# 384 columns of half the rows of one w_down tile, loaded earlier in 18 small transfers over a few DMA engines

## The chip, the cores and the metric

One core of a Trainium2 chip runs the kernel. The metric is the device time of one execution in microseconds, lower is better. Before the change three runs took 227.02, 227.11 and 227.11 us, so the median is 227.11 us.

## The reference

One token of a decoder layer with a parallel attention branch and feed-forward branch, all in fp32. Attention reads a window of 4096 cached keys and values of four key/value heads; the feed-forward part is a gated GELU.

```python
xn = _layernorm(x, axis=-1)                       # x: 1 x 1 x 1024
return x + _A_ref(xn, k_cache, v_cache, wq, wo) + _B_ref(xn, w_gate, w_up, w_down)
...
q = xn @ wq                                       # 1024 x 4096, 32 heads of 128
p = _softmax(q @ k.T * 128 ** -0.5, axis=-1)      # last 4096 rows of the caches
A = (p @ v) @ wo                                  # wo: 4096 x 1024
B = (gelu(xn @ w_gate) * (xn @ w_up)) @ w_down    # 1024 x 3584, w_down: 3584 x 1024
```

## The kernel before

**The work.** There is one token, so every weight is read once and used for one product of a vector and a matrix. The kernel is a stream of 94.38 MB from HBM through one buffer, `ring`, of 128 partitions by 32768 fp32 columns (128 KB of each partition). The table `PLAN` (line 269) gives the order of the loads, the column at which each starts, and the load whose readers must be done before it may be issued: wq in two halves, K and V of two heads, half of w_gate, K and V of the other two heads, the rest of w_gate, w_up in three parts, wo in two halves (`o 0`, `o 1`), and w_down in three parts (`d 0`, `d 1`, `d 2`). All of these loads are issued by SyncE (SP in the profile), in this order, by `load` (line 313); `used` (line 335) issues what stands behind a load once its consumer's instructions have been written. A DMA waits on SP until the readers of the columns that it overwrites are done, so a late reader holds the whole SP queue.

**A tile.** Rows of w_down and wo are laid out so that a partition holds whole neighbouring rows: `grouped` (line 292) puts row `p * rows + t` of a part into partition `p` as its tile `t`, 1024 columns wide. So w_down has 28 tiles: 16 in `d 0`, 8 in `d 1` and 4 in `d 2`. `PIECES` (line 27) cuts `d 1` into two transfers of 4 tiles each, and `d 2` into one of two tiles (24 and 25), one of tile 26, and two of half of tile 27. These six, and `d 0` in one piece, are the seven w_down transfers of the profile.

**Who consumes what.** A tile is either multiplied on TensorE (PE) by a column of `oz` or `hz`, accumulating in `out_p`, or on VectorE (DVE) by `add_scaled` (line 435): out_part = out_part + tile * column, one scalar per partition. In wo (`outputs`, line 697) even tiles go to PE and odd ones to DVE. In w_down (`downs`, line 707) the six tiles of `KEPT` in `d 0` go to DVE and all others to PE; `out_part` itself is summed over partitions by PE with `units` just ahead of tile 24. The last half tile goes to `last_p`, is added to `y` as `y_last`, and is stored.

**The hidden vector.** `hidden` (line 651) stands between the two halves of wo on PE and DVE: it turns the gated vector, which lies along rows of `copies` (tile `kT` in the profile), into columns of `hz`, one for each w_down tile, with 28 small matmuls into `tp` and seven DVE copies into `hz`.

**Synchronisation** is derived by the class `Flow`: it notes what each instruction reads and writes, and gives each the waits that it needs. Every instruction is issued from its line 238, so nearly every row of the profile has the line L238, and rows are told apart by their tiles.

Of the kernel before, what the change touches and what calls it, by code (L numbers as in the profile page):

```python
# [5 lines left out]
F32 = mybir.dt.float32  # L6
# [5 lines left out]
P = 128  # L12
D = 1024
# [4 lines left out]
DF = 3584  # L18
NR = 4
NJ = D // (NR * P)  # L20
NB = 512
# [10 lines left out]
GELU_C = math.sqrt(2.0 / math.pi)  # L32

ROW = (31, 32, 95, 96)
SIZES = {"tp": NB, "acc": 2 * NB, "part": 8 * NB, "rows": 2 * NB}


# [203 lines left out]
class Pool:  # L241
# [6 lines left out]
    def tile(self, shape, dtype, name, tag=None, bufs=1):  # L248
# [5 lines left out]
        if key not in self.made:  # L254
            alloc = self.nc.alloc_psum_tensor if self.space == "psum" else self.nc.alloc_sbuf_tensor
            width = SIZES.get(tag, size)
            self.made[key] = (alloc(f"{tag}_{n}", [P, width], dtype), width)
# [18 lines left out]
]  # L276

# [1 line left out]
def decode_layer(nc, x, k_cache, v_cache, wq, wo, w_gate, w_up, w_down, out):  # L279
    consts = stream = work = Pool(nc.nc, "sbuf")  # L280
    psum = Pool(nc.nc, "psum")

    def fours(w, jj):
        return w[NR * P * jj:NR * P * (jj + 1), :].rearrange("(p r) n -> p r n", r=NR)


    def windows(cache, i):
        pair = cache[0, 2 * i:2 * i + 2, SK - WIN:, :]
        return pair.rearrange("g (p j) d -> p g (j d)", p=P // 2)


    def grouped(w, start, rows):
        return w[start:start + P * rows, :].rearrange("(p t) n -> p t n", p=P)


    def source(kind, i):
        if kind == "q":
            return fours(wq, i)
        if kind == "g":
            return fours(w_gate, i)  # L300
        if kind[0] == "u":
            return fours(w_up, i)[:, {"u": slice(NR), "ua": slice(2), "ub": slice(2, NR)}[kind]]
        if kind in "kv":
            cache = k_cache if kind == "k" else v_cache
            return windows(cache, i)
        if kind == "o":
            return grouped(wo, P * WIDE * i, WIDE)
        return grouped(w_down, P * sum(DOWN[:i]), DOWN[i])

    ring = stream.tile([P, RING], F32, name="ring")  # L310
    loaded = {}

    def load(key, at):
        kind, i = key
        src = source(*key)
        if kind in "kv":

            loaded[key] = dst = ring[:, at:at + RING // 4]
            if kind == "v":
                nc.sync.dma_start(dst, src)  # L320
            else:
                for odd in range(2):
                    nc.sync.dma_start(dst[odd:P:2], src[:, odd])
            return
        rows, n = src.shape[1:]
        loaded[key] = ring[:, at:at + rows * n]
        dst = loaded[key].rearrange("p (t n) -> p t n", n=n)
        pieces = PIECES[i] if kind == "d" else (0, rows)
        for t, end in zip(pieces, pieces[1:]):
            cuts = 2 if key == ("d", 2) and end == rows else 1  # L330
            for cut in range(cuts):
                cols = slice(cut * n // cuts, (cut + 1) * n // cuts)
                nc.sync.dma_start(dst[:, t:end, cols], src[:, t:end, cols])

    def used(key):

# [12 lines left out]
    for c in (0, 2):  # L349
        nc.scalar.dma_start(  # L350
            x_out[ROW[c]:ROW[c] + 2, :].rearrange("c (h n) -> c h n", h=2), x_in[c:c + 2]
        )

    ident = consts.tile([P, P], F32, name="ident")
# [12 lines left out]

    hz = consts.tile([P, TD + 1, 32], F32, name="hz")
    nc.vector.memset(hz, 0.0)
    oz = consts.tile([P, HQ + 1, 32], F32, name="oz")  # L370
    nc.vector.memset(oz, 0.0)
    units = consts.tile([P, 2, 32], F32, name="units")
# [62 lines left out]
    def add_scaled(total, w, factor, first):  # L435

        if first:
            nc.vector.tensor_scalar(total, w, factor, None, op0=ALU.mult)
        else:
            nc.vector.scalar_tensor_tensor(total, w, factor, total, op0=ALU.mult, op1=ALU.add)  # L440
# [51 lines left out]
    m = work.tile([P, HKV], F32, name="m")  # L492
# [135 lines left out]
    copies = (h_sb[:, 0:4], h_sb[:, 4:6])  # L628
    rows = (P, 32 * (NA - 4))
# [21 lines left out]
    def hidden():  # L651

        h_p = small("h_p")
        kept = ((0, 16, 0, 4), (1, 8, 0, 2), (1, 4, 2, 1))
        t = at = 0
        for b, count, c, n in kept:
            k = rows[b]
            m = NB // count  # L660
            flat = copies[b][:k].rearrange("p a n -> p (a n)")
            for i in range(count):
                nc.tensor.matmul(
                    h_p[:, at + i:at + n * count:count], flat[:, i:P * count:count],
                    ident[:k, 32 * c:32 * (c + n):32], start=True, stop=True,
                )
            for own in range(n):
                r = slice(m * own, m * own + m)
                cols = slice(at + count * own, at + count * own + count)
                nc.vector.tensor_copy(hz[r, t:t + count, 31], h_p[r, cols])  # L670
            t, at = t + count, at + n * count


    out_p = psum.tile([P, CO], F32, name="out_p", tag="out")
    out_part = work.tile([P, D], F32, name="out_part")
# [5 lines left out]
    def store(h, rows):  # L681

        dst = out.rearrange("a b (h c n) -> h (a b c) n", h=2, c=4)[h]
        for queue, c in ((nc.sync, 0), (nc.scalar, 2)):
            stores.append(len(nc.ops))
            queue.dma_start(dst[c:c + 2], rows[ROW[c]:ROW[c] + 2, :])

    def accumulate(p, z, t, w, start, stop):
        w = w.rearrange("p (h c n) -> p c h n", c=4, n=CO // 2)
        z = z.rearrange("p t m -> p (t m)")  # L690
        for c in range(4):
            at = 32 * (t + c) + 31 - ROW[c]
            nc.tensor.matmul(
# [13 lines left out]
    def downs():  # L707

        nonlocal mark
        tiles = [loaded["d", i][:, n * D:(n + 1) * D] for i in range(3) for n in range(DOWN[i])]  # L710
        for t in KEPT:
            add_scaled(out_part, tiles[t], hz[:, t, 31:32], False)
        order = [t for t in range(DOWN[0]) if t not in KEPT]
        half = DOWN[0] + DOWN[1] // 2
        for t in [*order[:6], *range(DOWN[0], half), *order[6:], *range(half, TD - 4)]:
            accumulate(out_p, hz, t, tiles[t], False, False)
        accumulate(out_p, units, 0, out_part, False, False)
        for t in range(TD - 4, TD - 1):
            accumulate(out_p, hz, t, tiles[t], False, False)

        n = CO // 2
        t, wt = TD - 1, tiles[TD - 1]
        accumulate(out_p[:, :n], hz, t, wt[:, :NB], False, True)
        mark = len(nc.ops)
        nc.vector.tensor_add(y, out_p, x_out)
        store(0, y[:, :n])
        last_p = small("last_p")[:, :n]
        accumulate(last_p, hz, t, wt[:, NB:], True, True)
        nc.vector.tensor_add(y_last, y[:, n:], last_p)
        store(1, y_last)  # L730
# [4 lines left out]
    half = RING // 8  # L735
    for key, _, _ in PLAN:
        kind, i = key
        if kind == "q":
            project("q", i, loaded.pop(key), range(NR), 8)
        elif kind == "k":  # L740
            kn = loaded.pop(key)
            if i == 0:
                projected("q", 8)
                q_sb = query_rows()
            transpose_keys(2 * i, kn[:, :half], range(8), (1, 4, 6))
            if i == 0:
                queries(q_sb)

            s = scores(2 * i)
            transpose_keys(2 * i + 1, kn[:, half:], range(4), ())  # L750
            exponentials(2 * i, s)
            transpose_keys(2 * i + 1, kn[:, half:], range(4, 8), (4, 5, 7))
            s = scores(2 * i + 1)
        elif kind == "v":
            vn = loaded.pop(key)
            pT = transpose_probs(2 * i)
            exponentials(2 * i + 1, s)
            values(2 * i, pT, vn[:, :half])
            values(2 * i + 1, transpose_probs(2 * i + 1), vn[:, half:])
            if i == 1:  # L760
                maxima()
        elif kind == "g":
            project("g", i, loaded.pop(key), range(NR), NA)
            if i == 1:
                state = factors()
                projected("g", NA)
                gelu()
        elif kind in ("ua", "ub", "u"):
            taken = {"ua": (0, 1), "ub": (2, 3), "u": range(NR)}[kind]
            project("u", i, loaded.pop(key), taken, NA)  # L770
            if kind == "ua":
                normalizers(*state)
            elif kind == "ub":
                heads()
        elif kind == "o":
            if i == 0:
                projected("u", NA)
                gated()
            outputs(i)
            if i == 0:  # L780
                hidden()
        elif i == 2:
            downs()
        used(key)
# [26 lines left out]
```

## Time and profile before

| | |
|---|---|
| runs shown | 227.02, 227.11, 227.11 us; median 227.11 us |
| the profiled execution, its time | 227.12 us |
| its span, from first to last instruction | 225.2 us |
| mean granted TensorE clock | 0.795 |
| PE, DVE, ACT, POOL busy | 56%, 48%, 13%, 0% of the span |
| read from HBM | 94.38 MB, 419 GB/s over the span |

A row of the timeline gives the start and the length in us, then engine, line, operation, output tile and input tiles, shapes, how many instructions were merged, and in brackets how long the engine had been idle and what ended it. "PEld" is the weight load of a matmul, "SPq" is an instruction of SP's own sequencer such as the issue of a DMA. The windows view has one row for each stretch: its length, the busy time of each engine with the number of instructions in parentheses, the granted TensorE clock, the mean busy share of the core's 16 DMA engines, and GB/s. The share is made by the packets that start in the stretch, so a short stretch can be a few hundredths off. In the DMA view, q1 is the queue of SP's transfers, q10 that of ScalarE's, and "instruction" are the core's own fetches of instructions, which run on the same 16 engines.

### The profile page before, as it was taken

The page shows a single profiled execution, that of the slowest core. Times are in us where ns is not written, and L with a number is a line of the kernel's source. Part 1 is how long each engine was busy: PE and PEld are TensorE (multiplying, and loading weights), DVE is VectorE, ACT ScalarE, POOL GpSimd, SP SyncE. Part 2 cuts the span into 40 slices and gives each one's busy share as a digit, 9 for nine tenths or more (in the row PEclk, how much of TensorE's full clock was granted, in tenths as well). Part 3 has the DMA queues.
Part 4 walks back from the last instruction along what each step waited for, and adds up shares of the span by engine and source line. Part 5 has one row for each costly group of instructions (what it writes and reads, how often), then busy time and mean ns, then how long its engine had stood idle before and what let it go on. Part 6 is the DMA issues. An engine that isn't in the chain of part 4 may idle for free.

```text
span 225.2 us, 2481 instructions
## 1 busy us (share of the span) xinstructions
PE 125.4 (56%) x1107; PEld 66.0 (29%) x1107; DVE 107.7 (48%) x133; ACT 28.2 (13%) x54; POOL 0.7 (0%) x6
## 2 busy tenths in 40 slices
PE   0120910538799992999736553236308989700975
PEld 0010200103646651755511110001004887300441
DVE  7030920591215382345139589239608813950931
ACT  2020000002407410464300310000000000000000
POOL 1000000000000000000000000000000000000000
PEclk9999975596959999799988958558955755765699
DMA  9899889799997999998999999999999999998993
GB/s 373 373 396 536 372 384 547 343 402 463 438 489 336 432 439 451 402 516 377 461 390 418 433 463 418 479 422 466 399 442 454 407 442 442 410 442 361 425 404 141
DMA packets 2954, 94.52 MB, mean 420 GB/s; under 512 B 367, under 2 KB 383, under 8 KB 769
## 3 DMA queue, kind: packets, MB, share of 16 engines
q1 hardware_dynamic: 2920, 94.38, 97.5%
q8 instruction: 8, 0.13, 0.2%
q10 hardware_dynamic: 24, 0.01, 0.0%
q14 instruction: 2, 0.01, 0.0%
HBM read 94.38 MB, written 0.00 MB: 419 GB/s over the span
## 4 chain that ended last, share of the span: by engine, by line
DMA 68%; DVE 20%; PE 9%; ACT 1%; issue 1%; SPq 0%; DVEq 0%
DMA ring<-in_B_w_gate 26%; DMA ring<-in_A_wq 18%; DMA ring<-in_A_wo 13%; DVE part L238 13%; DMA ring<-in_B_w_down 11%; PE tp L238 6%; DVE out_part L238 3%; PE out L238 3%; DVE rows L238 2%; DVE g_sb L238 1%; ACT kT L238 1%; DVE hz L238 1%; PE acc L238 0%; DVE kT L238 0%; SPq L238 0%
## 5 line engine op out<-in xcount | busy, mean ns | idle before, releaser
L238 PE MATMUL acc<-ring,xz 128*32 128x512 f32 x176 | 31.5, 811 | 39.4 <-DMA ring<-in_A_wq 22.3
L238 DVE SCALAR_TENSOR_TENSOR part<-ring,xz,part 128x3584 f32<-128x3584 f32 (+1 forms) x9 | 37.2, 4129 | 23.2 <-DMA ring<-in_A_wq 12.5
L238 PEld LDWEIGHTS acc<-ring,xz 128*32 128x32 f32 x176 | 7.1, 139 | 59.6 <-issue 25.6
L238 PE MATMUL tp<-ident,ring 128*128 128x128 f32 x128 | 20.9, 308 | 6.2 <-DMA ring<-in_A_k_cache 4.0
L238 PE MATMUL out<-ring,hz 128*32 128x256 f32 (+1 forms) x176 | 12.3, 426 | 14.2 <-DMA ring<-in_B_w_down 14.0
L238 PEld LDWEIGHTS tp<-ident,ring 128*128 128x128 f32 x128 | 15.5, 156 | 15.7 <-DMA ring<-in_A_k_cache 4.9
L238 DVE SCALAR_TENSOR_TENSOR out_part<-ring,oz,out_part 128x1024 f32<-128x1024 f32 x15 | 19.3, 1284 | 0.5
L238 DVE COPY kT<-tp 128x512 f32<-128x512 f32 x12 | 8.2, 690 | 20.0 <-PE tp L238 20.0
L238 PE MATMUL out<-ring,oz 128*32 128x256 f32 x128 | 12.1, 562 | 9.5 <-DMA ring<-in_A_wo 9.5
L238 ACT ACTIVATE kT<-tp 128x512 f32<-128x512 f32 x20 | 11.6, 596 | 25.8 <-PE tp L238 25.5
L238 PE MATMUL tp<-ident,kT 128*128 128x4 f32 (+2 forms) x56 | 13.1, 366 | 1.3 <-DVE hz L238 1.3
L238 PEld LDWEIGHTS tp<-ident,kT 128*128 128x128 f32 (+1 forms) x56 | 12.8, 319 | 1.9 <-DVE hz L238 1.5
L238 PE MATMUL acc<-part,units 128*32 128x512 f32 x44 | 7.2, 741 | 9.2 <-DVE part L238 9.2
L238 PEld LDWEIGHTS out<-ring,hz 128*32 128x32 f32 x176 | 5.7, 123 | 21.0 <-DMA ring<-in_B_w_down 17.0
L238 DVE SCALAR_TENSOR_TENSOR out_part<-ring,hz,out_part 128x1024 f32<-128x1024 f32 x6 | 7.7, 1285 | 8.0 <-DMA ring<-in_B_w_down 7.8
L238 DVE TENSOR_SCALAR part<-ring,xz 128x3584 f32<-128x3584 f32 (+1 forms) x3 | 6.5, 2171 | 10.4 <-DMA ring<-in_A_wq 7.4
L238 PEld LDWEIGHTS out<-ring,oz 128*32 128x32 f32 x128 | 5.4, 160 | 16.1 <-DMA ring<-in_A_wo 10.4
L238 PE MATMUL s<-kT,qz 128*32 128x512 f32 x64 | 9.4, 714 | 0.0
L238 DVE TENSOR_REDUCE m<-s 128x2 f32<-128x1024 f32 x4 | 4.9, 1224 | 7.5 <-PE s L238 7.5
L238 PE MATMUL o<-ring,pT 128*32 128x128 f32 x256 | 7.8, 274 | 1.0 <-ACT pT L238 1.0
L238 PEld LDWEIGHTS o<-ring,pT 128*32 128x32 f32 x256 | 6.7, 110 | 1.9 <-ACT pT L238 1.9
L238 PE MATMUL tp<-ident,x_rows 2*128 2x2 f32 x4 | 0.6, 252 | 10.5 <-DMA x_rows<-in_A_x 10.5
(88 smaller groups left out, 68.9 us busy)
## 6 DMA issues: line engine op xcount, KB each, us to landing
ring<-in_B_w_gate SPq DMA_DIRECT2D x2, 7168.0 KB, 29.5
ring<-in_A_k_cache SPq DMA_DIRECT2D x4, 2048.0 KB, 18.1
ring<-in_A_v_cache SPq DMA_DIRECT2D x2, 4096.0 KB, 25.3
ring<-in_B_w_up SPq DMA_DIRECT2D x2, 3584.0 KB, 22.5
ring<-in_B_w_up SPq DMA_DIRECT2D x1, 7168.0 KB, 26.0
ring<-in_B_w_down SPq DMA_DIRECT2D x2, 2048.0 KB, 21.6
ring<-in_B_w_down SPq DMA_DIRECT2D x1, 1024.0 KB, 23.9
ring<-in_B_w_down SPq DMA_DIRECT2D x1, 512.0 KB, 24.8
```

Of the source, the lines that this page charges most:

```text
L238: return lambda *a, **k: self.flow.issue(self.engine, lambda: call(*a, **k))
```

## The change

Tile 25, the third last, has 1024 columns in each partition. Of its 64 odd partitions the last 384 columns (1536 bytes each) no longer come with the tile.

- The first transfer of `d 2` (two tiles, 128 partitions by 2048 columns) becomes two: 64 even partitions by 2048 columns, and 64 odd partitions by 1664. The missing 384 columns in `ring` are set to zero by a memset on GpSimd (POOL), on all partitions, ahead of them.
- The 64 rows of 1536 bytes go to a new tile `moved`, of 128 partitions by 3 slots by 384. `load_moved` issues them on SP behind the second half of wo, in 18 transfers: five of 5 rows and thirteen of 3 rows. A table `MOVED` says which rows go to which partitions, in steps of four partitions, all below partition 52.
- `hidden` gets six more matmuls and six DVE copies, which pick the 64 scalars of these rows into `moved_h`, on the partitions where the rows now lie.
- `downs` gets three `add_scaled` on DVE, on 52 partitions by 384 columns, one for each slot, ahead of the six `KEPT` ones.
- `moved` and `moved_h` are cleared on POOL at the start.

```diff
+MC = 384
+MOVED = ((0, 0, 0, 20, 4), (0, 1, 20, 12, 4), (1, 0, 32, 12, 4), (1, 1, 44, 12, 4),
+         (2, 0, 56, 5, 1), (2, 1, 61, 3, 1))
...
-    (("o", 0), 0, ("ub", 0)), (("o", 1), 16384, ("u", 1)),
+    (("o", 0), 0, ("ub", 0)), (("o", 1), 16384, ("u", 1)), (("m", 0), None, ("u", 1)),
...
+        if key == ("d", 2):
+            end = 2 * n - MC
+            nc.gpsimd.memset(loaded[key][:, end:2 * n], 0.0)
+            both = src[:, 0:2].rearrange("p t n -> p (t n)")
+            nc.sync.dma_start(loaded[key][0:P:2, :2 * n], both[0:P:2])
+            nc.sync.dma_start(loaded[key][1:P:2, :end], both[1:P:2, :end])
+            pieces = pieces[1:]
...
+    def load_moved():
+        rest = w_down[DF - 4 * P:, D - MC:].rearrange("(r x) n -> x r n", x=8)[5]
+        for s, a, first, count, step in MOVED:
+            for j in range(step):
+                to = 32 * a + j
+                nc.sync.dma_start(
+                    moved[to:to + 4 * (count // step):4, s], rest[first + j:first + count:step]
+                )
...
+    nc.gpsimd.memset(moved, 0.0)
+    nc.gpsimd.memset(moved_h, 0.0)
...
+        for s, a, first, count, step in MOVED:
+            end = min(8 * first + 5 + 40 * step, NB)
+            taken = flat[:, 8 * first + 5:end:2 * step]
+            n = taken.shape[1]
+            nc.tensor.matmul(
+                h_p[32 * a:32 * a + n, at + s:at + s + 1], taken, ident[:k, 64:65],
+                start=True, stop=True,
+            )
+            nc.vector.tensor_copy(
+                moved_h[32 * a:32 * a + n, s:s + 1], h_p[32 * a:32 * a + n, at + s:at + s + 1]
+            )
...
+        for s in range(3):
+            add_scaled(out_part[:52, D - MC:], moved[:52, s], moved_h[:52, s:s + 1], False)
         for t in KEPT:
```

**SP, from the second half of wo to the last piece of w_down.** A row of SP is one transfer: tile and source, partitions by columns, and what it waits for. Before:

```order
L238 DMA ring<-in_A_wo 128x16384 [waits flow_e_PE,flow_e_DVE] x2
L238 DMA ring<-in_B_w_down 128x16384 [waits flow_e_PE,flow_e_DVE]
L238 DMA ring<-in_B_w_down 128x4096 [waits flow_e_PE,flow_e_DVE] x2
L238 DMA ring<-in_B_w_down 128x2048 [waits flow_e_PE,flow_e_DVE]
L238 DMA ring<-in_B_w_down 128x1024 [waits flow_e_PE]
L238 DMA ring<-in_B_w_down 128x512 [waits flow_e_DVE]
```

And now:

```order
L241 DMA ring<-in_A_wo 128x16384 [waits flow_e_PE,flow_e_DVE] x2
L241 DMA moved<-in_B_w_down 5x384 [waits flow_e_Pool]
L241 DMA moved<-in_B_w_down 5x384 x3
L241 DMA moved<-in_B_w_down 3x384 x12
L241 DMA moved<-in_B_w_down 5x384
L241 DMA moved<-in_B_w_down 3x384
L241 DMA ring<-in_B_w_down 128x16384 [waits flow_e_PE,flow_e_DVE]
L241 DMA ring<-in_B_w_down 128x4096 [waits flow_e_PE,flow_e_DVE] x2
L241 DMA ring<-in_B_w_down 64x2048 [waits flow_e_PE,flow_e_Pool]
L241 DMA ring<-in_B_w_down 64x1664
L241 DMA ring<-in_B_w_down 128x1024 [waits flow_e_PE]
L241 DMA ring<-in_B_w_down 128x512 [waits flow_e_DVE]
```

The 18 small transfers stand behind wo and ahead of `d 0`; the first transfer of `d 2` is split by even and odd partitions, and waits for POOL where it waited for DVE.

**DVE, from the copies into hz to the first w_down tiles.** Before:

```order
L238 COPY hz<-tp 64x8 [waits flow_e_PE]
L238 COPY hz<-tp 64x8
L238 COPY hz<-tp 128x4 [waits flow_e_PE]
L238 SCALAR_TENSOR_TENSOR out_part<-ring,oz,out_part 128x1024 [waits flow_d_606]
L238 SCALAR_TENSOR_TENSOR out_part<-ring,oz,out_part 128x1024 [waits flow_e_DVE] x7
L238 SCALAR_TENSOR_TENSOR out_part<-ring,hz,out_part 128x1024 [waits flow_d_691,flow_e_DVE]
```

And now:

```order
L241 COPY hz<-tp 128x4 [waits flow_e_PE]
L241 COPY moved_h<-tp 20x1 [waits flow_e_Pool,flow_e_PE]
L241 COPY moved_h<-tp 20x1 [waits flow_e_PE] x4
L241 COPY moved_h<-tp 10x1 [waits flow_e_PE]
L241 SCALAR_TENSOR_TENSOR out_part<-ring,oz,out_part 128x1024 [waits flow_d_608]
L241 SCALAR_TENSOR_TENSOR out_part<-ring,oz,out_part 128x1024 [waits flow_e_DVE] x7
L241 SCALAR_TENSOR_TENSOR out_part<-moved,moved_h,out_part 52x384 [waits flow_d_613,flow_d_612,flow_d_614,flow_d_611,flow_d_615,flow_d_610,flow_d_616,flow_d_609,flow_e_DVE]
L241 SCALAR_TENSOR_TENSOR out_part<-moved,moved_h,out_part 52x384 [waits flow_d_621,flow_d_620,flow_d_622,flow_d_619,flow_d_623,flow_d_618,flow_d_624,flow_d_617,flow_e_DVE]
L241 SCALAR_TENSOR_TENSOR out_part<-moved,moved_h,out_part 52x384 [waits flow_d_626,flow_d_625,flow_e_DVE]
L241 SCALAR_TENSOR_TENSOR out_part<-ring,hz,out_part 128x1024 [waits flow_d_723,flow_e_DVE]
```

Six copies, each waiting for PE, stand ahead of the second half of wo, and three short additions, which wait for the small transfers, ahead of the first w_down tile.

**PE, at the same place.** Before:

```order
L238 MATMUL tp<-ident,kT 128x2 x7
L238 MATMUL tp<-ident,kT 128x1 [waits flow_e_DVE]
L238 MATMUL tp<-ident,kT 128x1 x3
L238 MATMUL out<-ring,oz 32x256 [waits flow_d_606]
L238 MATMUL out<-ring,oz 32x256 x31
```

And now:

```order
L241 MATMUL tp<-ident,kT 128x1 [waits flow_e_DVE]
L241 MATMUL tp<-ident,kT 128x1 x3
L241 MATMUL tp<-ident,kT 20x1 [waits flow_e_DVE] x5
L241 MATMUL tp<-ident,kT 10x1 [waits flow_e_DVE]
L241 MATMUL out<-ring,oz 32x256 [waits flow_d_608]
L241 MATMUL out<-ring,oz 32x256 x31
```

Each of the six new matmuls waits for the DVE copy ahead of it, and each new copy for its matmul, so the two engines take turns ahead of wo's second half.

More of the change, by code (lines that the diff above doesn't have):

```diff
@@ L314, in load @@
         kind, i = key
+        if kind == "m":
+            load_moved()
+            return
         src = source(*key)
@@ L333, in load @@
                 nc.sync.dma_start(dst[:, t:end, cols], src[:, t:end, cols])
+    moved = consts.tile([P, 3, MC], F32, name="moved")
+    moved_h = consts.tile([P, 3], F32, name="moved_h")
+    def load_moved():
[6 more added lines that the diff above has]
+                )
     def used(key):
@@ L671, in hidden @@
             t, at = t + count, at + n * count
+        k = rows[1]
+        flat = copies[1][:k, 0]
+        for s, a, first, count, step in MOVED:
[9 more added lines that the diff above has]
+            )
     out_p = psum.tile([P, CO], F32, name="out_p", tag="out")
@@ L737, in decode_layer @@
         kind, i = key
+        if kind == "m":
+            continue
         if kind == "q":
```

## The prediction, on record before the changed kernel was run

> **What bounds the kernel now.** I read the page first: the busy line of the DMA engines, and the queues.
>
> ```profile
> DMA  9899889799997999998999999999999999998993
> ...
> q1 hardware_dynamic: 2920, 94.38, 97.5%
> q8 instruction: 8, 0.13, 0.2%
> ```
>
> The 16 DMA engines are busy from the first slice to the last but one, and SP's own queue fills 97.5% of them, while the busiest compute engine stands at 56%. So time is bytes over rate, and any edit matters only by what it does to the DMA engine that ends last. The chain of waits, in order of time, tells how it ends:
>
> ```profile
> 196.56 1.30 DVE out_part L238
> 197.86 0.02 issue
> 197.87 0.33 SPq L238
> 198.20 0.04 issue
> 198.24 24.72 DMA ring<-in_B_w_down
> 222.96 0.04 issue
> 223.00 0.47 PE tp L238 x8
> 223.47 0.02 issue
> 223.50 0.29 DVE y_last L238
> ```
>
> The last transfer is issued at 198.24 us and lands at 222.96: it lies 24.7 us behind other transfers. The steps of the chain ahead of 198 us therefore don't set the time; they could be late by many us. The 0.83 us of PE and DVE behind the landing, and the store, are as they were. The windows view then shows how the engines run dry:
>
> ```profile
> 220.60:220.80 0.20, 0.20 (x8) 0.11 (x12) 0.00 (x0) 0.00 (x0) 0.00 (x0) 1.00 0.96 369
> 220.80:221.00 0.20, 0.20 (x12) 0.12 (x8) 0.00 (x0) 0.00 (x0) 0.00 (x0) 1.00 0.70 266
> 221.00:221.20 0.20, 0.20 (x12) 0.09 (x4) 0.00 (x0) 0.00 (x0) 0.00 (x0) 1.00 0.55 205
> ...
> 221.80:222.00 0.20, 0.20 (x5) 0.11 (x8) 0.00 (x0) 0.00 (x0) 0.00 (x0) 1.00 0.50 195
> 222.00:222.20 0.20, 0.20 (x8) 0.00 (x0) 0.00 (x0) 0.00 (x0) 0.00 (x0) 1.00 0.53 205
> 222.20:222.40 0.20, 0.20 (x8) 0.03 (x4) 0.00 (x0) 0.00 (x0) 0.00 (x0) 1.00 0.23 82
> ```
>
> The last two numbers are the DMA share and GB/s. The share is 0.96 until 220.8, then stands between 0.50 and 0.55 (elsewhere in this stretch up to 0.63), and falls at about 222.3. Some 7 or 8 of the 16 engines are done at about 220.9, the other 8 or 9 at about 222.3: **two groups, 1.4 us apart**. Why is plain from the instruction fetches. One of the eight falls into the microsecond from 216.9 to 217.9:
>
> ```profile
> q8 instruction: 1, 0.02, 6.8%
> ```
>
> 6.8% of 16 engines for 1 us is 1.09 us on one engine. Eight such fetches, if each falls on another engine, leave about half of the engines over a us behind, which fits the two groups.
>
> **The change on the DMA engines.** Its bytes are those of before; they are dealt out anew. Rate first: transfers of 64 rows (the K loads) fill all engines like those of 128:
>
> ```profile
> 42.00:51.00 9.00, 4.92 (x32) 1.12 (x32) 8.91 (x2) 0.00 (x0) 0.00 (x0) 0.85 0.99 426
> ```
>
> 426 / (16 x 0.99) = 26.9 GB/s, or 26.9 bytes per ns, for each engine. The 64 odd rows that get shorter are four on each engine if they are dealt out evenly, as that row says: 4 x 1536 / 26.9 = 228 ns less on every engine. Against it stands one transfer more, that is one completion packet. Its nearest price is in the stretch of the two last stores, 224.54 to 224.62:
>
> ```profile
> DMA packets 8, 0.00 MB, mean 26 GB/s; under 512 B 4, under 2 KB 8, under 8 KB 8
> ...
> q10 hardware_dynamic: 4, 0.00, 5.6%
> ```
>
> Four packets of q10, two of 512 bytes and two completions, take 0.056 x 16 x 80 = 72 ns: 36 ns for one of each, of which 512 / 26.9 = 19 ns are the bytes; so 17 ns at most for a packet's fixed part and a completion together, and 9 taken for the completion. **An engine that gets no small transfer ends 0.22 us earlier.**
>
> The small ones are 13 transfers of 3 rows and 5 of 5 rows, a row an engine by their description. If they always go to the same first three or five, three engines get 18 rows and two get 5. One row with its completion: 1536 / 26.9 + 17 = 74 ns. From below it is 57 ns, bytes alone. From above, by the packets of 2048 bytes that alone run at 221.8: 195 / (16 x 0.50) = 24.4 bytes per ns, 84 ns a packet, with 9 for a completion 93. I take 74, which is a packet of the same kind with its bytes added. So the three engines get 18 x 74 = 1.33 us (1.03 to 1.67) and lose 0.22: 1.1 us more (0.8 to 1.45). The two get 5 x 74 - 220 = 0.15 us more. The early group was 1.4 us ahead of the late one, which now ends 0.22 us earlier. So if the three are in the early group, they end 1.4 - 0.22 - 1.1 = 0.1 us ahead of the late ones (0.4 ahead to 0.3 behind, by the two ends), and the late group sets the end, at 222.96 - 0.22.
>
> **The change on SP.** 18 issues more, between the second half of wo and `d 0`:
>
> ```profile
> 158.11 0.33 SPq L238 DMA_DIRECT2D ring<-in_A_wo  x1
> 179.52 0.33 SPq L238 DMA_DIRECT2D ring<-in_B_w_down  x1
> ...
> 26.49 1.17 SPq L238 DMA_DIRECT2D ring<-in_A_k_cache  x2
> ```
>
> At 0.33 to 0.59 us each (the dearest row, two in 1.17) they take 5.9 to 10.6 us, and SP idles from 158.4 to 179.5. Their memset on POOL is long done then: 128x128 took 0.20 us there, nine times the columns 1.8.
>
> ```profile
> 0.73 0.20 POOL L238 MEMSET ident<- 128x128 f32 x1 [0.29 <-POOLq L799]
> ```
>
> **The change on PE and DVE.** Six rounds of matmul, copy and two handovers stand ahead of wo's second half:
>
> ```profile
> 187.82 2.03 PE L238 MATMUL tp<-ident,kT 96*128 96x1 f32 x8 [0.45 <-DVE hz L238]
> 189.78 6.12 PE L238 MATMUL out<-ring,oz 128*32 128x256 f32 x64
> 189.89 0.17 DVE L238 COPY hz<-tp 128x4 f32<-128x4 f32 x1 [2.12 <-PE tp L238]
> 189.97 10.52 DVE L238 SCALAR_TENSOR_TENSOR out_part<-ring,oz,out_part 128x1024 f32<-128x1024 f32 x8
> 208.21 4.58 PE L238 MATMUL out<-ring,hz 128*32 128x256 f32 x48 [12.31 <-DMA ring<-in_B_w_down]
> 208.26 7.89 DVE L238 SCALAR_TENSOR_TENSOR out_part<-ring,hz,out_part 128x1024 f32<-128x1024 f32 x6 [7.78 <-DMA ring<-in_B_w_down]
> ```
>
> Four matmuls of this kind took 2.03 us (eight records), 0.51 each; with 0.17 for the copy and about 0.07 for the handovers a round is at most 0.75, six 4.5 us; the weights are narrower now (20 columns), so perhaps 3. PE's second half of wo starts 3 to 4.5 us later and ends by 200.4; DVE's ends by 205. The three additions behind it, at 1284 ns x 384 / 1024 = 0.48 us,
>
> ```profile
> L238 DVE SCALAR_TENSOR_TENSOR out_part<-ring,oz,out_part 128x1024 f32<-128x1024 f32 x15 | 19.3, 1284 | 0.5
> ```
>
> make 1.5 us and with some 18 waits, at a few hundredths each, end by 207.5. Both engines sat idle until 208.2 for `d 0` (12.31 and 7.78 us), so nothing shows. What these readers release is late by as much: the first piece of `d 1`, and `d 2` behind it with the POOL memset (128x384, three times 0.20). The last issue moves from 198.2 to about 204. PE starts on `d 0` at 208.2, when its last engine has landed, and the early ones are 1.4 us and a little more ahead of that: `d 0` feeds them until about 206, and the 4 MB of `d 1` at 426 GB/s for over 9 us more. So every issue still comes ahead of its turn; the cover is 8 us for `d 1` and over 10 for `d 2`. If it were gone, each us of delay would be a us of empty DMA engines.
>
> [...] The two last pieces, 256 KB each, reach PE at
>
> ```profile
> 222.37 0.16 PEld L238 LDWEIGHTS out<-ring,hz 128*32 128x32 f32 x8 [0.46 <-DMA ring<-in_B_w_down]
> 223.00 0.16 PEld L238 LDWEIGHTS tp<-ring,hz 128*32 128x32 f32 x8 [0.47 <-DMA ring<-in_B_w_down]
> ```
>
> 0.63 us apart, and their bytes alone are 0.61. So a transfer in a full queue costs an engine hundredths of a us. [...]
>
> **The sum.** 227.12 (the profiled execution, 0.01 above the median) - 0.22 = **226.9 us**, 0.1% less. A difference of 0.2%, 0.45 us, is about what a measurement of this kernel tells from none; I call that "same".
>
> **Rivals.**
> - *One of the three engines is in the late group* (slower side). The 18 rows then come on top of the last end: 222.96 + 1.1, so 227.12 + 1.1 = 228.2 us (227.9 to 228.6). It decides once an engine's lead is below about 1 us. For it: 9 of 16 are late, and no view names the engine of a packet. Against it: strung together, each packet of an engine starting where the one before ended, the trace's packets put the two engines that carried ScalarE's one- and two-row transfers of x at the start into the early group; a transfer of three rows should take these two and one more. [...] 0.16.
> - *The load is right but too large, or one of the two five-row engines is late*: a row costs 93 ns, or 0.15 us comes on top of the end. 226.95 to 227.4, taken as 227.1. 0.10.
> - *It doesn't do what it says*: the small transfers spread over all engines, each gets its four rows back with four completions and 18 x 9 ns at most. 227.1 to 227.3. 0.04.
> - *SP can't have 20 transfers under way.* The profile shows seven at most (the w_down issues up to 198.24, with `d 0` not landed before 208). If SP stalls until the second half of wo lands (issued 158.11, median 30.7 us to landing, 188.8), `d 0` comes 2 to 3 us too late: 229.5. 0.05.
> - *Each small transfer holds its engine until it has landed*: 1.4 us at most, what the last store has from its issue at 223.81 to the end of the span at 225.2; 18 x 1.4 - 1.4 = 24 us more, 251 us. The two pieces 0.63 us apart speak against it. 0.02.
> - *More is gained*, because the late engines also lose fetch time: 226.4. 0.04.
>
> ```profile
> 223.81 0.26 SPq L238 DMA_DIRECT2D out_y<-y_last  x1
> ...
> ring<-in_A_wo SPq DMA_DIRECT2D x1, 30.7
> ```
>
> **How the numbers follow.** The forecast has 0.59. Within 0.2%: 0.59 + 0.10 + 0.04 = 0.73. Slower: 0.16 + 0.05 + 0.02 = 0.23. Faster by more: 0.04. The forecast's own range is 226.7 to 227.1. With the second and third rival it holds 0.73, too little, so the range reaches over the first rival too, to 228.3: 0.73 + 0.13 = 0.86.
>
> **What would show it.** Right: the share of the DMA engines in the last two us falls in one step, not in two, or by a smaller one; the last piece lands at about 222.7; PE's idle time ahead of `d 0` shrinks by 3 to 4.5 us and the row's start at 208.2 stays; SP's 18 issues end before 179.5. Wrong: the last landing at 223.5 or later with a share of about 3 of 16 (0.2) ahead of it (first rival), or an issue of `d 0` behind 179.5 that waits for no reader (the stall).

## The result, and the profile after

The changed kernel takes **227.96 us** (median of seven runs, 227.67 to 228.06) beside 227.11 us of the kernel before (seven runs, 227.02 to 227.21): 1.0034 times, 95% interval 1.0022 to 1.0046. The prediction was 226.9 us with 0.73 on "same"; the time lies in its range (226.7 to 228.3), but the change is slower by more than the bound of 0.2%. The profiled execution took 227.99 us, with a span of 226.0 us.

The busy line and the queue on the page tell nothing of it; the DMA engines are as full as before:

```profile
DMA  9889889899999999998999998999999999998992
...
q1 hardware_dynamic: 3064, 94.38, 97.4%
```

The end of the chain of waits after:

```profile
192.92 1.29 DVE out_part L241
...
200.84 1.30 DVE out_part L241
202.29 21.40 DMA ring<-in_B_w_down
223.73 0.47 PE tp L241 x8
224.22 0.29 DVE y_last L241
```

The last transfer is issued 4.0 us later than before (202.29 for 198.24), as the work ahead of it suggests, and still lies 21.4 us behind others. It lands at 223.69 us, 0.73 later than before. That is most of the difference of the two profiled executions, 0.87 us. The rest of this section is where these 0.73 us came from. The timeline of PE has one row for each stretch of w_down:

```profile
209.15 4.08 PE L241 MATMUL out<-ring,hz 128*32 128x256 f32 x48 [10.21 <-DMA ring<-in_B_w_down]
214.07 3.66 PE L241 MATMUL out<-ring,hz 128*32 128x256 f32 x64 [0.83 <-DMA ring<-in_B_w_down]
218.97 1.93 PE L241 MATMUL out<-ring,hz 128*32 128x256 f32 x32 [1.24 <-DMA ring<-in_B_w_down]
221.25 1.07 PE L241 MATMUL out<-ring,hz 128*32 128x256 f32 x16
...
223.73 0.43 PE L241 MATMUL tp<-ring,hz 128*32 128x128 f32 x8 [0.20 <-DMA ring<-in_B_w_down]
```

Before, the first row began at 208.21 and the last at 223.00. So the delay is complete in the first row: `d 0`, the first transfer behind the 18 small ones, is a whole 0.94 us later. It stays like that, and the last row is 0.73 late, since the transfer that was cut is shorter. The windows view shows how many engines are late:

```profile
221.60:221.80 0.20, 0.20 (x12) 0.12 (x8) 0.00 (x0) 0.00 (x0) 0.00 (x0) 1.00 0.80 307
221.80:222.00 0.20, 0.20 (x12) 0.04 (x4) 0.00 (x0) 0.00 (x0) 0.00 (x0) 1.00 0.69 266
222.00:222.20 0.20, 0.20 (x8) 0.00 (x0) 0.00 (x0) 0.00 (x0) 0.00 (x0) 1.00 0.53 205
222.20:222.40 0.20, 0.12 (x4) 0.00 (x0) 0.00 (x0) 0.00 (x0) 0.00 (x0) 1.00 0.38 143
222.40:222.60 0.20, 0.12 (x4) 0.12 (x8) 0.00 (x0) 0.00 (x0) 0.00 (x0) 1.00 0.16 61
222.60:222.80 0.20, 0.20 (x8) 0.04 (x5) 0.00 (x0) 0.00 (x0) 0.00 (x0) 1.00 0.24 92
222.80:223.00 0.20, 0.20 (x8) 0.00 (x0) 0.00 (x0) 0.00 (x0) 0.00 (x0) 1.00 0.08 31
223.00:223.20 0.20, 0.20 (x8) 0.10 (x8) 0.00 (x0) 0.00 (x0) 0.00 (x0) 1.00 0.08 31
```

The next to last number, the DMA share, stays at 0.7 to 0.8 until 222.0, where before half of the engines had been done since 220.9. Most are done at about 222.4, and a share of 0.08 to 0.24 goes on until 223.2: one to four engines, where three were loaded with 18 rows each.

What should be hidden was hidden. SP, PE, DVE and POOL, in order of time:

```profile
158.59 12.75 SPq L241 DMA_DIRECT2D moved<-in_B_w_down  x18
179.63 23.09 SPq L241 DMA_DIRECT2D ring<-in_B_w_down  x8
...
190.12 0.24 PE L241 MATMUL tp<-ident,kT 96*20 96x1 f32 x2 [0.26 <-DVE hz L241]
190.40 0.15 DVE L241 COPY moved_h<-tp 20x1 f32<-20x1 f32 x1 [0.33 <-PE tp L241]
190.60 0.24 PE L241 MATMUL tp<-ident,kT 96*20 96x1 f32 x2 [0.24 <-DVE moved_h L241]
...
192.92 10.53 DVE L241 SCALAR_TENSOR_TENSOR out_part<-ring,oz,out_part 128x1024 f32<-128x1024 f32 x8
199.54 0.42 POOL L241 MEMSET ring<- 128x384 f32 x1 [197.21 <-DVE out_part L241]
203.48 1.90 DVE L241 SCALAR_TENSOR_TENSOR out_part<-moved,moved_h,out_part 52x384 f32<-52x384 f32 x3
...
209.20 3.92 DVE L241 SCALAR_TENSOR_TENSOR out_part<-ring,hz,out_part 128x1024 f32<-128x1024 f32 x3 [3.82 <-DMA ring<-in_B_w_down]
```

The 18 issues end at 171.3, 8 us ahead of the issue of `d 0` at 179.63, which came at 179.52 before. Six rounds take from 190.12 to 192.92, and DVE sits idle for 3.82 us ahead of `d 0`.

### The profile page after: what moved, and what is told of

Its sections match the earlier page's. It is cut to its first block, busy times and chain, and to the rows that moved or that the text cites. A ratio compares the mean times of both kernels' runs of the same rounds, so it can differ in the third digit from the quotient of the medians.

```text
span 226.0 us, 2547 instructions
## 1 busy us (share of the span) xinstructions
PE 125.2 (55%) x1119; PEld 66.3 (29%) x1119; DVE 110.4 (49%) x142; ACT 28.0 (12%) x54; POOL 2.2 (1%) x9
## 4 chain that ended last, share of the span: by engine, by line
DMA 67%; DVE 21%; PE 10%; ACT 1%; issue 1%; SPq 0%; DVEq 0%
DMA ring<-in_B_w_gate 26%; DMA ring<-in_A_wq 18%; DMA ring<-in_A_wo 13%; DVE part L241 13%; DMA ring<-in_B_w_down 9%; PE tp L241 7%; DVE out_part L241 4%; PE out L241 3%; DVE rows L241 2%; DVE g_sb L241 1%; ACT kT L241 1%; DVE hz L241 1%; PE acc L241 0%; DVE moved_h L241 0%; DVE kT L241 0%
## 5 line engine op out<-in xcount | busy, mean ns | idle before, releaser
L241 PE MATMUL acc<-ring,xz 128*32 128x512 f32 x176 | 32.5, 845 | 39.3 <-DMA ring<-in_A_wq 22.6
L241 PE MATMUL out<-ring,hz 128*32 128x256 f32 (+1 forms) x176 | 11.8, 413 | 12.4 <-DMA ring<-in_B_w_down 12.4
L241 PE MATMUL tp<-ident,kT 128*128 128x4 f32 (+4 forms) x68 | 14.5, 334 | 2.8 <-DVE hz L241 1.6
L241 PEld LDWEIGHTS tp<-ident,kT 128*128 128x128 f32 (+3 forms) x68 | 13.7, 283 | 3.9 <-DVE hz L241 1.8
L241 PE MATMUL s<-kT,qz 128*32 128x512 f32 x64 | 7.7, 598 | 0.0
```

Of the source, the lines that this page charges most:

```text
L241: return lambda *a, **k: self.flow.issue(self.engine, lambda: call(*a, **k))
```

## The experiments

Four theories could explain 0.94 us on `d 0`. **A**: small transfers that follow one another on the same engines are dear by their number. **B**: the rows are dear by their bytes, or an engine among the three was late from the start (the first two rivals). **C**: the partitions that they write. **D**: the split of the transfer of `d 2`, or the work on PE and DVE. A start of PE on `d 0` at 208.2 us is that of before, and 209.15 that of the change. All ratios are to the kernel before, measured beside each version; it took 227.2 us each time (medians of 227.17 to 227.20).

**The two halves of the change.** `cut_only` takes the entry of the small transfers out of the plan, so that nothing is loaded into `moved`:

```diff
-    (("o", 0), 0, ("ub", 0)), (("o", 1), 16384, ("u", 1)), (("m", 0), None, ("u", 1)),
+    (("o", 0), 0, ("ub", 0)), (("o", 1), 16384, ("u", 1)),
```

> Leaves out the 18 small transfers (the 384 columns of the odd rows of tile 25 never arrive, so their products are missing); the split of the first d 2 transfer, the memset, the six extra matmuls and copies and the three additions stay. Both theories (the three engines were slowed by the number of small transfers, or by the number of their rows) have all 16 engines end 0.22 us earlier: 226.9 us, PE starts on d 0 at 208.2. A rival that puts the loss into the split, the memset or the later hidden vector expects 227.5 to 228.

Measured: 227.02 us, 0.9990 (0.9980 to 0.9999). PE's rows for `d 0` and for the last piece:

```profile
208.21 4.20 PE L241 MATMUL out<-ring,hz 128*32 128x256 f32 x48 [9.82 <-DMA ring<-in_B_w_down]
...
222.78 0.43 PE L241 MATMUL tp<-ring,hz 128*32 128x128 f32 x8 [0.20 <-DMA ring<-in_B_w_down]
```

`d 0` is where it was, and the last row begins 0.22 us earlier than before. `load_only` keeps the small transfers and takes the cut back, so that these rows come twice:

```diff
-        if key == ("d", 2):
+        if False:
```

> Keeps the 18 small transfers and all compute, but doesn't cut tile 25 (the products of these rows are added twice). Both theories: the load alone makes the loss, without the 0.22 us that the cut gives back: 228.2 us, PE starts on d 0 at 209.1 as in the changed kernel. If the loss sat in the split: 227.1 to 227.3.

Measured: 228.06 us, 1.0041 (1.0026 to 1.0056).

```profile
209.15 9.03 PE L241 MATMUL out<-ring,hz 128*32 128x256 f32 x112 [10.55 <-DMA ring<-in_B_w_down]
...
223.95 0.43 PE L241 MATMUL tp<-ring,hz 128*32 128x128 f32 x8 [0.21 <-DMA ring<-in_B_w_down]
```

The same 209.15, and 0.22 us more at the end than with the cut. The two halves add up to the change, and D falls: the loss is the 18 transfers.

**The same rows in fewer transfers.** `six_transfers` brings the 64 rows in six transfers, up to four rows for each partition, over the same three and five engines (the rows then lie on other partitions than their scalars):

```diff
-    moved = consts.tile([P, 3, MC], F32, name="moved")
+    moved = consts.tile([P, 4, MC], F32, name="moved")
...
-        for s, a, first, count, step in MOVED:
-            for j in range(step):
-                to = 32 * a + j
...
+        for to, n, parts, slots in (
+            (0, 0, 5, 4), (1, 20, 5, 1), (2, 25, 3, 4), (3, 37, 3, 4), (32, 49, 3, 4), (33, 61, 3, 1)
+        ):
+            rows_ = rest[n:n + parts * slots].rearrange("(p s) n -> p s n", p=parts)
+            nc.sync.dma_start(moved[to:to + 4 * parts:4, 0:slots], rows_)
```

> The same 64 rows of 1536 bytes on the same engines (18 rows on each of three, 5 on each of two), but in 6 transfers instead of 18, of up to 4 rows an engine (the rows lie on other partitions than their scalars, so these products are wrong). Theory A, a price for each transfer, about 0.07 us for its completion beside 0.06 for a row: 18 x 0.06 + 6 x 0.07 - 0.22 = 1.3 us on the three engines, just within their lead of 1.4, so 226.9 to 227.1 us and d 0 at about 208.2. Theory B, a price for each row of 0.13 us: no change from the changed kernel, 228.0 us and d 0 at 209.1.

Measured: 227.12 us, 1.0001 (0.9991 to 1.0011).

```profile
208.12 4.32 PE L241 MATMUL out<-ring,hz 128*32 128x256 f32 x48 [9.65 <-DMA ring<-in_B_w_down]
```

`spread_six` keeps the 18 transfers and puts three each behind six big ones:

```diff
...
+    (("ua", 0), 0, ("k", 1)), (("m", 0), None, ("k", 1)),
+    (("ub", 0), 8192, ("v", 1)), (("m", 1), None, ("v", 1)),
+    (("u", 1), 16384, ("g", 1)), (("m", 2), None, ("g", 1)),
+    (("o", 0), 0, ("ub", 0)), (("m", 3), None, ("ub", 0)),
+    (("o", 1), 16384, ("u", 1)), (("m", 4), None, ("u", 1)),
+    (("d", 0), 0, ("o", 0)), (("m", 5), None, ("o", 0)),
...
+        for s, to, at, end, step, n in jobs[3 * group:3 * group + 3]:
```

> The changed kernel with its 18 small transfers in six threes, each behind another large load (from the first part of w_up to d 0), all else equal. If a small transfer costs 0.13 us wherever it stands: 228.0 us. If the price is one of completions that follow each other closely, large packets between them hide it: 18 x 0.07 = 1.3 us, 226.9 to 227.0 us, and d 0 at 208.2.

Measured: 227.03 us, 0.9994 (0.9984 to 1.0003).

```profile
208.14 4.35 PE L241 MATMUL out<-ring,hz 128*32 128x256 f32 x48 [9.59 <-DMA ring<-in_B_w_down]
```

In both the engines carry the rows and bytes of the change, and nothing is late; in `six_transfers` they stand at the same place too. So the 18 rows fit into the lead of these engines, and B falls in both its forms. What costs is 18 transfers in a row.

**How many in a row.** `two_nines` puts nine behind the first half of wo and nine behind the second:

```diff
...
+    (("o", 0), 0, ("ub", 0)), (("m", 0), None, ("ub", 0)),
+    (("o", 1), 16384, ("u", 1)), (("m", 1), None, ("u", 1)),
...
+        for s, to, at, end, step, n in jobs[9 * group:9 * group + 9]:
```

> The same 18 transfers of the same rows to the same places, nine behind the first half of wo and nine behind the second half. Theory A in its backlog form (about a dozen small transfers in a row go at the price of their packets, and only those behind them are dear): neither nine is dear, the product of the first tile of w_down starts at 208.2 us in the trace, time 226.9 to 227.1 us. Theory A in its per-follower form (every small transfer that follows another on the same engines costs about 0.06 us more than its packets): 16 of 18 still follow one, start at 209.0 to 209.1, time 227.8 to 228.0. Rival B (each row is dear wherever it stands, by its bytes): 228.0, as with the 18 together.

Measured: 227.19 us, 1.0019 (1.0000 to 1.0038). The ten runs scatter from 227.03 to 228.79, but their spans do not (225.1 to 225.4 us; the shortest of the change's seven was 225.8): the scatter lies outside the kernel's instructions, and the trace is the better witness:

```profile
208.31 8.97 PE L241 MATMUL out<-ring,hz 128*32 128x256 f32 x112 [10.41 <-DMA ring<-in_B_w_down]
```

`d 0` is 0.10 us late rather than 0.94. `halves` goes the other way, with each row in two transfers of 192 columns, 36 in a row:

```diff
-                nc.sync.dma_start(
-                    moved[to:to + 4 * (count // step):4, s], rest[first + j:first + count:step]
-                )
+                for half in (slice(0, MC // 2), slice(MC // 2, MC)):
+                    nc.sync.dma_start(
+                        moved[to:to + 4 * (count // step):4, s, half],
+                        rest[first + j:first + count:step, half],
+                    )
```

> Each of the 18 transfers is cut into two of half the columns (192), so 36 transfers stand in a row, with the same rows, bytes and engines. Theory A (the number of transfers in a row sets the cost): with some fourteen cheap ones and 0.30 us for each one behind them the 36 take 7.5 us rather than 2.3, so the first tile's product starts at 212 to 214 us and the time is 231 to 233 us; with 0.13 us for each of them it starts at 211.5 and the time is 230.3. Rival B (rows or bytes set the cost): the start stays at 209.1 to 209.4 and the time at 228.0 to 228.3.

Measured: 231.39 us, 1.0184 (1.0170 to 1.0198).

```profile
158.47 26.99 SPq L241 DMA_DIRECT2D moved<-in_B_w_down  x36
185.56 16.98 SPq L241 DMA_DIRECT2D ring<-in_B_w_down  x8
...
212.14 4.16 PE L241 MATMUL out<-ring,hz 128*32 128x256 f32 x48 [13.44 <-DMA ring<-in_B_w_down]
```

The same bytes cost 2.99 us more, (212.14 - 209.15) / 18 = 0.17 us for each further transfer. (The issue of `d 0` moves to 185.56, still 3 us ahead of the landing of wo's second half, issued at 158.09 with 30.7 us to landing, so the queue did not run dry.) `narrow_rows` is the reverse: 18 transfers with 96 columns each.

```diff
-                    moved[to:to + 4 * (count // step):4, s], rest[first + j:first + count:step]
+                    moved[to:to + 4 * (count // step):4, s, 0:96],
+                    rest[first + j:first + count:step, 0:96]
```

> The 18 transfers bring 96 of the 384 columns, a quarter of the bytes; the cut of the big transfer stays, so the products of 288 of the moved columns are left out. Theory A (ends of transfers in a row, about 0.175 us apart on the same engines whatever they carry, with four or five of them hidden): first tile's product still from 208.9 to 209.3, time 227.8 to 228.1 us. Rival B (bytes of the rows, a quarter of them): 208.2 and 227.0 to 227.1.

Measured: 227.90 us, 1.0030 (1.0018 to 1.0042), beside the changed kernel again:

> The changed kernel once more, as the yardstick beside the others of this call: 227.8 to 228.1 us, first tile's product from 209.0 to 209.2.

Measured: 228.07 us, 1.0048 (1.0028 to 1.0069), with `d 0` used from 209.00. And `narrow_rows`:

```profile
209.18 9.02 PE L241 MATMUL out<-ring,hz 128*32 128x256 f32 x112 [10.52 <-DMA ring<-in_B_w_down]
```

A quarter of the bytes, and the delay of the full rows. **A is shown**: what transfers in a row cost goes by their number. Eighteen cost the same with rows of 384 and of 1536 bytes, and each further one (768 bytes) 0.17 us on each engine it uses.

**Where the time goes.** The DMA view of a stretch so short that one packet starts in it gives the length of that packet, share x 16 x stretch. Four such stretches, in this order: in the changed kernel a row in the middle of the 18 (187.05 to 187.06), one of the last rows (187.91 to 187.92) and the first 64 KB of `d 0` right behind such a string (188.26 to 188.30); and in `narrow_rows` the first 64 KB behind one, with one completion (187.31 to 187.34; a completion is the packet of 4 bytes that stands behind each transfer's rows on an engine, 14.1% x 16 x 4 ns = 9 ns for the one at 186.953 to 186.957 of the change).

```profile
q1 hardware_dynamic: 1, 0.00, 40.6%
q1 hardware_dynamic: 1, 0.00, 108.8%
q1 hardware_dynamic: 1, 0.07, 505.6%
q1 hardware_dynamic: 2, 0.07, 939.2%
```

They took 65 ns, 174 ns, 3.24 us and 4.50 us, where 64 KB usually take 2.42 (25.2% of 16 engines for 0.6 us, for the one that starts between 169.9 and 170.5). Strung together, each packet starting where the one before on its engine ended, the change's packets show the same on each of the three engines: 14 rows at 0.067 us each with their completions, four at 0.17 to 0.18, and then 0.82 to 0.89 us more for the 64 KB packet behind, together 2.5 to 2.6 us. The narrow rows are all cheap (0.025 us each), but the packet behind them takes 2.0 us more, together 2.4 to 2.5. The 36 halves take 5.6 to 5.8 us, and each nine of `two_nines` 0.9 to 1.0. So part of the price falls on the packet behind the string, and the small packets alone don't show it. What takes this time, and why the narrow rows themselves stay cheap, no run here shows.

**Where they write.** `high_partitions` moves them to partitions from 64 on:

```diff
-                to = 32 * a + j
+                to = 64 + 32 * a + j
...
+            add_scaled(out_part[64:116, D - MC:], moved[64:116, s], moved_h[64:116, s:s + 1], False)
```

> The 18 transfers write the partitions from 64 on rather than those from 0 on, and the three additions read those, with scalars that are zero there: the products of the moved rows are left out of the output. [...] Theory A (the number of transfers in a row): unchanged, 227.9 to 228.1 us, first tile's product from 209.1.

Measured: 228.46 us, 1.0056 (1.0042 to 1.0070); `d 0` at 210.08 in the trace. This is no result that A foresaw: 0.5 us more than the change. `own_partitions` was to make each engine write only its own partitions:

```diff
-                    moved[to:to + 4 * (count // step):4, s], rest[first + j:first + count:step]
...
+            to, s = i % 8, i // 8
+            nc.sync.dma_start(moved[to:to + 8 * n:8, s], rest[at:end:step])
```

> The 18 transfers write partitions j, j + 8, j + 16 and so on (j from 0 to 7, three slots) rather than j, j + 4, j + 8, so that, if the engines are taken in order, each of them writes only the eight partitions that it also fills in the big transfers; the moved rows then meet other rows' scalars, so their products are left out of the right sum. Theory A (ends in a row): unchanged, first tile's product from 209.0 to 209.2, time 227.8 to 228.1 us. Rival C (an engine that writes into partitions which another engine is filling waits for it, and holds it up; for it speaks that the run with partitions from 64 on was 0.5 us slower than the changed kernel): 208.2 and 227.0 us, or in between if both have a part.

Measured: 228.40 us, 1.0051 (1.0036 to 1.0066), `d 0` at 209.38. No placement brought the 0.94 us back, so C doesn't explain them. Both other placements seem to cost something on top: the intervals of `own_partitions` and of the changed kernel beside it (`after_again`) overlap, but its `d 0` is 0.38 us later than there. In these two runs the trace's 64 KB packets of all engines that run beside the small ones take 2.5 to 3.6 us, where 2.42 is usual; in the changed kernel only three do, which start behind the small ones (3.2 to 3.3). No view shows which engine writes which partition, so that steps of 8 are the engines' own partitions was my assumption, and the run tests another placement, no more. The two runs took 0.33 and 0.50 us more than the changed kernel (228.07 and 227.96); why, no run here shows.

**A version that was to be faster.** The late group's engines could be relieved without small rows. `eight_engines`, from the kernel before, splits the first transfer of `d 2`; `rows_112` is the control with the same bytes on all engines:

```diff
+        if key == ("d", 2):
+            for rows_ in (slice(0, 112), slice(112, 120), slice(120, 128)):
+                nc.sync.dma_start(dst[rows_, 0:2], src[rows_, 0:2])
+            pieces = pieces[1:]
...
+            for rows_ in (slice(0, 112), slice(112, 128)):
```

> The kernel before, with no row moved to other partitions. The first transfer of the last tile but two is split: partitions 0 to 111 (seven on each engine), and the other 16 in two transfers of eight partitions each, which should go to eight engines, the lowest-numbered. Those eight then get two rows of 8 KB of these 16 rows, the other eight none. If the late group of engines are the others (by packets strung together they are), these end 8192 / 26.9 = 0.30 us earlier and the two groups close from 1.4 us to 0.8: last landing at 222.66, time 226.8 us (0.13% less). If the late group is not the upper eight: 0.3 us more, 227.4 us. If transfers of a few rows behind each other are dear even at two, 227.0 to 227.2.

> The kernel before, the first transfer of the last tile but two split into partitions 0 to 111 and 112 to 127, so that all engines carry the same bytes, seven rows and one. If the 4.6 us of the run with eight engines came from the two transfers of eight partitions: 227.1 to 227.3 us. If they came from the transfer of 112 partitions (seven to an engine rather than eight, so that engines fill partitions that others fill): 231 to 232 us.

Measured: 231.79 us, 1.0203 (1.0178 to 1.0228), and 231.12 us, 1.0186 (1.0156 to 1.0216). The windows of `rows_112`:

```profile
212.00:214.00 2.00, 1.79 (x36) 0.86 (x32) 1.93 (x3) 0.00 (x0) 0.00 (x0) 1.00 0.98 418
216.00:218.00 2.00, 0.63 (x12) 0.13 (x4) 0.01 (x1) 0.00 (x0) 0.00 (x0) 1.00 1.13 246
218.00:220.00 2.00, 0.41 (x4) 0.20 (x8) 0.00 (x0) 0.00 (x0) 0.00 (x0) 0.70 0.90 186
220.00:222.00 2.00, 2.00 (x24) 0.96 (x20) 0.00 (x0) 0.00 (x0) 0.00 (x0) 0.50 1.01 238
222.00:224.00 2.00, 2.00 (x20) 0.58 (x12) 0.00 (x0) 0.00 (x0) 0.00 (x0) 0.50 0.97 229
224.00:226.00 2.00, 1.74 (x24) 0.84 (x24) 0.00 (x0) 0.00 (x0) 0.00 (x0) 0.60 0.57 219
```

The DMA engines stay busy and move half: 186 to 246 GB/s where it was 418. At 224 it is over: 219 / (16 x 0.57) = 24 bytes per ns and engine, as for the last pieces before (24.4). The imbalance doesn't do it, since `rows_112` has none. The transfer of 112 partitions does: its first rows start at 215.4 us in the trace, and the 16 KB packets of `d 1` beside them grow from 0.62 us to 0.9 and then 1.25 by 217.3, before any engine has carried its seven rows. So the idea of relieving eight engines wasn't tested by this, and which eight engines the two small transfers took no view shows.

No version that brings the moved rows beats the kernel before by a measurable amount. The best of them is `spread_six`, which gives back what the change lost and is level with before; and `cut_only`, which pays nothing for the rows, puts what such a move can gain at about 0.1%.

## Why the prediction was wrong, step by step

- **Bound by the DMA engines, two groups 1.4 us apart:** held, and the three engines were in the early group. Strung together, the packets of the change have the three end wo's second half between 186.5 and 186.8 us and the last engine of the late group at 188.5, so they were 1.7 to 2.0 us ahead of that one. That the 18 transfers load the same three engines was an assumption; the strings bear it out, with 18 rows on each of three.
- **The cut, 0.22 us less on every engine:** right. `cut_only` against before at the last row: 223.00 - 222.78 = 0.22; `load_only` against the change: 223.95 - 223.73 = 0.22.
- **Three engines with 18 rows, each with its completion 74 ns, 1.33 us (1.03 to 1.67): this step failed.** The sum of 18 equal prices left out what a string leaves behind. The first 14 rows were a little cheaper than I had them (0.067 us), the last four cost 0.17 to 0.18, which makes 1.66 to 1.69 us, at the upper end of my bounds. But the 64 KB packet behind them took 0.82 to 0.89 us more, a term that I had put at nothing. The 18 cost 2.5 to 2.6 us, more than the lead of the three, and the last of these packets ended at 191.80 us where the last of the other engines ended its own at 190.91: 0.89 late, beside 0.94 on `d 0`. With 2.5 in the place of 1.33 the prediction's own sum gives 222.96 - 1.4 - 0.22 + 2.5 = 223.8 for the last landing; it was 223.69. The right engines were named and the direction of the load was right; the size of one term, and with it the conclusion "0.1 us ahead of the late ones", was wrong.
- **Why the term was too small:** I priced a packet and its completion from transfers of which each engine carried one or two, and from bytes. Those rows hold no long string. The bound "from above" (93 ns) was another rate of bytes, so both ends left this out. The runs show that the price goes by the number in a row: 36 cost 5.6 to 5.8 us, 18 2.4 to 2.6, nine 0.9 to 1.0. An estimate through these, 0.175 us for each less 0.65, gives 5.65, 2.5 and 0.9; for six threes, or the six larger transfers, the rows alone make more, an estimated 18 x 0.067 = 1.2 us, which is within the three engines' lead: `d 0` came at 208.14 and 208.12. What in the chip takes the 0.17 us was not tried; theory A is about the number, not about its cause.
- **"A transfer in a full queue costs hundredths of a us" (from the two pieces 0.63 us apart):** true of those pieces, but no evidence here. Each of them keeps every engine busy for 0.6 us, longer than 0.17, so such a price cannot show. My estimate is that it shows when a transfer gives an engine less than 0.17 us of bytes, by the prediction's 26.9 bytes per ns some 4.6 KB; a row of the change is a third of it. Fewer transfers did help: with six in place of 18 the time went from 227.96 to 227.12.
- **The two engines with five rows more, 0.15 us:** each took 0.34 us for its five rows. One of the two was in the late group, but 0.8 us ahead of its last engine, so nothing shows.
- **SP:** 0.71 us an issue (12.75 / 18) and not 0.33 to 0.59, above my bounds, but covered: the 36 of `halves` took 27 us and still ended ahead of need.
- **PE and DVE, POOL:** six rounds 2.8 us (3 to 4.5), three additions 1.9 (1.5), the memset 0.42 (0.6). All hidden; the last issue 4.0 us later, not 6.
- **Rivals:** the first (one of the three late) gave 228.2, close to the time, and the sign that I named for it, a share of about 0.2 ahead of the last landing, was there too. Yet `six_transfers` refutes it: the same engines with the same rows cost nothing, and the packets have all three in the early group. That the time lies in the range is luck: the range was stretched to 228.3 for this rival, whose mechanism did not occur. A sign that a mis-sized load gives as well told nothing of the two apart. A stalled SP and an engine held for 1.4 us did not occur.

## What to carry to other kernels

In these runs a transfer's price in a full queue had two parts on each engine, its bytes and a floor for each transfer (0.17 us for each further one, from the 36 of `halves` beside the 18 of the change), and the estimate that the larger one counts fits them: so count transfers per engine, not only bytes. The floor can hide in the packet that stands behind the row (4.50 us in `narrow_rows` where 2.42 is usual), so price the row with it. Small transfers showed no such cost three at a time behind big ones (`spread_six`, `d 0` at 208.14), or merged (`six_transfers`, 208.12; before, 208.21). And a price taken from rows in which nothing queues isn't an upper bound for rows that do: 93 ns was the most I had for a row with its completion, and 18 took 2.5 to 2.6 us, 0.14 each.

## What the runs showed of the hardware, unexpected

- A row of small transfers on the same engines cost by its number: 0.17 us for each further one (`halves`, 768 bytes), and 18 with 384 bytes as much as 18 with 1536 (`d 0` at 209.18 and 209.15). In the packets of the change 14 went at 65 ns for 1536 bytes, the other four took 0.17 to 0.18 us, and the 64 KB packet behind took 3.24 to 3.31 us rather than 2.42, or 4.4 to 4.5 behind 18 of 384 bytes.
- From one issue on SP to the next it took 0.71 us for transfers of three or five rows (12.75 / 18, in the change); the issue of wo's second half, of 128 rows, took 0.33, and that of `d 0` 0.33 to 0.35 (before and in `halves`).
- A transfer of 112 partitions in place of 128 halved what all engines moved (418 to some 186 to 246 GB/s in `rows_112`; 164 to 205 from 217 to 223 us in `eight_engines`), for some 8 us, until about the time that its last rows had landed. Whether that comes from the partitions that each engine writes or from the order of reads in memory, no run here shows.
